# GpSimd's sums of activations split into rows of 384 columns

## The chip, the cores and the metric

The kernel runs on one core of a Trainium2 chip. The metric is the device time of one execution in microseconds; the time before is the median of three runs.

## What is computed

Routing attention, followed by one MLP-mixer block, all in float32:

```
q, k, v: (4, 8, 768, 64); 16 centroids for each head
mask   = argmax(q_n @ c_n) == argmax(k_n @ c_n)          # routed clusters
attn   = softmax(where(mask, q @ k.T / 8, -1e9)) @ v
x      = attn, heads joined                              # (4, 768, 512)
u      = x + (relu(x.T @ w_tok1) @ w_tok2).T             # tokens: 768 -> 256 -> 768
out    = u + relu(u @ w_ch1) @ w_ch2                     # channels: 512 -> 1536 -> 512
```

## The kernel before

The kernel handles 16 pairs of heads (scores, values, place), then the token part of the mixer, then its channel part. The change touches the channel part alone, some 420 us to the end of the span.

**The channel part.** The four batches form two groups of two. For each group channel1 computes the hidden activations and channel2 the output. Both are products of 2 x 2 block matrices done in Strassen's way: seven block products for four, and in each of the seven again seven steps (function product). A step is a product of three blocks of 128 rows, of 384 columns each, on TensorE; each block takes two passes, so a step is six matmul instructions. What the Strassen scheme needs beside that are sums and differences of blocks: of the weights (prepared earlier, kept in DRAM as wd1 and wd2 and loaded through a ring of eight buffers), of the right-hand operand (tsum inside product, combine between products), and of the results (in the drain from PSUM, whose second operand is the sum so far).

**Shapes.** A Mat is a matrix with n rows of 768 columns in each partition; sub(a, c) is one of its four quarters, n/2 rows of 384 columns. The operands of channel1 are quarters of u, with n = 2, so a quarter is one row of 384. The hidden matrices Hm[...] have n = 6, so a quarter is three rows of 384: 1152 elements in each partition.

**Which engine.** Drains of PSUM are on VectorE (tt, line 868) or ScalarE (copy, line 848). The sums in the arena, the one large SBUF tile, go through the same tt: on GpSimd for channel1's sums and for the input sums of channel2's first two products (product is called with sums ("POOL",)), on VectorE for the others. In channel1 the combines of T1 and T2 may go to either engine in the first group. ScalarE applies relu in place (line 875). The function check (lines 1771 to 1804) counts on VectorE whether the inputs were in the fast path's range; it is issued in the program between channel1(1) and channel2(1), and two matmuls of three columns in it stand on TensorE's queue at that place.

**The order.** Every operation is handed to a planner, Program (g.add), with its modelled cost, the keys that it reads and writes (pieces of 32 words of the arena, PSUM banks) and the engines that may take it. TensorE's order is that of the program. For the others, plan repeatedly takes the earliest possible start and, among what an engine can start then, the operation with the earliest due time; due times are computed backwards from TensorE's. VectorE and GpSimd operations that touch no PSUM exclude each other in the model (the field port). Modelled cost is a + b x elements: GpSimd 0.12 + 0.0023 n, VectorE 0.16 + 0.00104 n. Each engine then executes its instructions in that order, with semaphores.

The planner's choice for VectorE, which may start an operation up to 0.15 us after the earliest one that it could start:

```python
                        if s > t + HOLD.get(e, 0.0) + 1e-9:
                            continue
                        ...
                        if pick is None or (o.due, o.seq) < (pick[0].due, pick[0].seq):
                            pick = (o, s)
```

Of the kernel before, what the change touches and what calls it, by code (L numbers as in the profile page):

```python
# [14 lines left out]
ALU = mybir.AluOpType  # L15
# [15 lines left out]
HS = HJ * P  # L31
# [678 lines left out]
def kernel(  # L710
# [112 lines left out]
    def bank(*i):  # L823
        return [("ps", n) for n in i]


    def mm(dst, lhsT, rhs, start, stop, cost, rd, wr, pos=None, tr=None):
        def fn(e):
            nc.tensor.matmul(  # L829
                dst, lhsT=lhsT, rhs=rhs, start=start, stop=stop, tile_position=pos,  # L830
                is_transpose=tr, skip_group_check=True,
            )

        return g.add({"PE": cost}, fn, rd, wr)
# [6 lines left out]
    def cost(kind, n):  # L841
        a, b = COST[kind]
        return a + b * n

    def copy(dst, src, n, rd, wr, engines=("ACT", "DVE")):
        def fn(e):
            if e == "ACT":
                nc.scalar.copy(out=dst, in_=src)  # L848
            else:
                nc.vector.tensor_copy(out=dst, in_=src)  # L850

        return g.add({e: cost(e, n) for e in engines}, fn, rd, wr)
# [13 lines left out]
    def tt(dst, a, b, op, n, rd, wr, engines=("DVE",)):  # L866
        def fn(e):
            (nc.vector if e == "DVE" else nc.gpsimd).tensor_tensor(out=dst, in0=a, in1=b, op=op)  # L868

        return g.add({e: cost(e, n) for e in engines}, fn, rd, wr)  # L870
# [13 lines left out]
    def dma(dst, src, rd, wr, kb, row, after=0.0, queue="SP"):  # L884

        q = {"SP": nc.sync, "ACT": nc.scalar, "POOL": nc.gpsimd}[queue]
        return g.add(
            {queue: ISSUE}, lambda e: q.dma_start(dst, src), rd, wr, (kb * 1024, row), after  # L888
        )
# [667 lines left out]
    def combine(dst, a, b, op, engines=("DVE",)):  # L1557

        n = dst.n // 2
        for i in range(2):  # L1560
            for c in range(2):
                (d, dk), (x, xk), (y, yk) = (z.sub(i, c) for z in (dst, a, b))
                tt(d, x, y, op, n * HS, xk + yk, dk, engines)

    def combine_rows(dst, a, b, op, parts=1):
        n = dst.n // parts
# [4 lines left out]
    def product(which, Q, X, dst, base, sums=None, then=()):  # L1571


        nonlocal nring, nt
        wide = which == 1
        sums = sums or (("POOL",) if wide else ("DVE",))
        ts = (t1s if wide else t2s)[nt % 2]
        nt += 1
        half = X.n // 2
        x = {(a, c): X.sub(a, c) for a in range(2) for c in range(2)}  # L1580

        def tsum(i, a, b):
            tt(ts[i].ap, a[0], b[0], ALU.subtract, half * HS, a[1] + b[1], ts[i].k(), sums)
            return ts[i].ap, ts[i].k()

        T1 = tsum(0, x[0, 1], x[0, 0])
        T2 = tsum(1, x[1, 1], T1)
        T3 = tsum(2, x[1, 1], x[0, 1])
        T4 = tsum(3, x[1, 0], T2)
        if wide:  # L1590
            sets = ((0, 3), (3, 6)) if nset[0] % 2 == 0 else ((3, 6), (0, 3))
        else:
            a = 2 * (nset[1] % 4)
            sets = ((a, a + 1), (a + 1, a + 2))
        nset[0 if wide else 1] += 1

        seq = (
            (0, x[0, 0], 0, True, (0, 0), False), (4, T1, 1, True, (1, 1), False),
            (5, T2, 0, False, (0, 1), False), (2, x[1, 1], 1, False, (0, 1), True),
            (6, T3, 0, False, (1, 1), True), (1, x[1, 0], 1, True, (0, 0), True),  # L1600
            (3, T4, 0, False, (1, 0), False),
        )
        for n, (pn, (r, rk), st, fresh, part, more) in enumerate(seq):
            w = ring[nring % len(ring)]
            nring += 1
            qi = (0, 1, 6, 2, 3, 4, 5)[Q]
            src = wd1[qi, pn] if wide else wd2[qi, pn].rearrange("p a c -> p (a c)")
            dma(
                w.ap.rearrange("p a c -> p (a c)"), src,
                [("wd", which, pn, s) for s in range(6)], w.k(), 192, 1536,  # L1610
            )
            b0, b1 = sets[st]
            for i in range(3):
                bk = b0 + i if wide else b0
                mm(
                    ps[:, bk, 0:HS], w.ap[:, i], r[:, 0] if wide else r[:, i],
                    fresh and (wide or i == 0), wide or i == 2, 0.64, w.k() + rk, bank(bk),
                )
            d, dk = dst.sub(*part)
            src = ps[:, b0:b1, 0:HS]  # L1620
            bks = bank(*range(b0, b1))
            sz = (b1 - b0) * HS
            src_base = dst if more else base
            if src_base is None:
                copy(d, src, sz, bks, dk)
            else:
                y, yk = src_base.sub(*part)
                tt(d, src, y, ALU.add, sz, bks + yk, dk)
            for late in dict(then).get(n, ()):
                late()  # L1630
# [7 lines left out]
    def channel1(grp):  # L1638
        u = {(K, N): Mat(uTs[2 * grp + N], 2 * K, 2) for K in range(2) for N in range(2)}
        Hm = {mn: Mat(t, 0, 6) for mn, t in Hs.items()}  # L1640
        T1, T2, T3, T4 = (Mat(t, 0, 2) for t in TL)
        a, b, c, h11 = Hm[0, 1], Hm[1, 0], Hm[1, 1], Hm[0, 0]
        SUB, ADD = ALU.subtract, ALU.add
        first = ("DVE", "POOL") if grp == 0 else ("POOL",)
        product(1, 0, u[0, 0], h11, None)
        combine(T1, u[0, 1], u[0, 0], SUB, first)
        combine(T2, u[1, 1], T1, SUB, first)
        product(1, 4, T1, c, None)
        product(1, 5, T2, a, h11)
        combine(T3, u[1, 1], u[0, 1], SUB, ("POOL",))  # L1650
        product(1, 6, T3, b, a)
        combine(a, a, c, ADD, ("POOL",))
        combine(c, c, b, ADD, ("POOL",))
        relu_of(c)
        product(1, 1, u[1, 0], h11, h11)
        relu_of(h11)
        product(1, 2, u[1, 1], a, a)
        relu_of(a)
        combine(T4, u[1, 0], T2, SUB, ("POOL",))
        product(1, 3, T4, b, b)  # L1660
        relu_of(b)
# [247 lines left out]
```

## Time and profile before

| | before |
|---|---|
| median of 3 runs | 811.82 us (810.64 to 812.14) |
| profiled execution | 812.03 us, span 810.2 us |
| TensorE busy | 791.3 us, 3743 matmuls |
| VectorE busy | 678.1 us |
| ScalarE busy | 473.0 us |
| GpSimd busy | 178.8 us, 124 instructions |
| mean granted TensorE clock | 0.998 |

The profile calls TensorE PE, VectorE DVE, ScalarE ACT, GpSimd POOL and SyncE SP. A row of the instructions in order of time has the start in us, the duration, the engine, the line, the operation, out<-in, the form (partitions x elements), how many were merged into it and, in brackets, the idle time before it with what ended it. An operation that is held up after its start shows a long duration and no idle time. A row of the busy time by stretch gives the stretch, its length, and for TensorE, its weight loads, VectorE, ScalarE and GpSimd the busy time and the instructions, then the granted clock, the DMA share and GB/s. The span is from the first to the last instruction; the execution's own time is 1.8 us longer.

### The profile page before, as it was taken

What the parts mean: (1) busy time and instruction counts of PE and PEld (TensorE: products, weight loads), DVE (VectorE), ACT (ScalarE), POOL (GpSimd) and SP (SyncE); (2) the same over time, 40 slices, a digit from 0 to 9 for tenths busy, and PEclk for the clock granted to TensorE, in tenths of its full rate; (3) what the DMA queues carried; (4) which work ended last, traced back from release to release, by engine and by line L of the source; (5) the groups of instructions that cost most, each with busy time, mean ns of one, the idle gap of its engine ahead of it and who ended that gap; (6) DMA issues with size and microseconds to landing.
All of it is one profiled execution on the core that took longest, in us unless ns stands there. A gap on an engine that the chain in (4) does not pass through costs nothing.

```text
span 810.2 us, 10859 instructions
## 1 busy us (share of the span) xinstructions
PE 791.3 (98%) x3743; PEld 429.2 (53%) x3743; DVE 678.1 (84%) x873; ACT 473.0 (58%) x612; POOL 178.8 (22%) x124
## 2 busy tenths in 40 slices
PE   5999999999999999999999999999999999999997
PEld 3444445554444445444555555555555555555554
DVE  3789999999999999998898867699975686789984
ACT  3688888888888875699913236433464504400424
POOL 1000000000000000000345398500196379620000
PEclk9999999999999999999999999999999999999999
DMA  5777778879888984369739765556899833333766
GB/s 123 213 181 179 179 195 207 211 181 226 204 210 182 226 236 115 82 132 222 146 85 260 202 199 177 184 176 202 239 252 239 223 109 107 97 96 99 160 156 167
DMA packets 265120, 143.49 MB, mean 177 GB/s; under 512 B 184289, under 2 KB 260961, under 8 KB 265057
## 3 DMA queue, kind: packets, MB, share of 16 engines
q1 hardware_dynamic: 262560, 141.88, 68.7%
q10 hardware_dynamic: 2496, 0.84, 0.4%
q8 instruction: 32, 0.52, 0.3%
q14 instruction: 32, 0.25, 0.1%
HBM read 91.95 MB, written 28.61 MB: 149 GB/s over the span
## 4 chain that ended last, share of the span: by engine, by line
PE 95%; DVE 1%; issue 1%; DMA 0%; ACT 0%; SPq 0%; ACTq 0%
PE ps L829 95%; DVE arena L868 0%; DVE arena L850 0%; DMA arena<-arena 0%; ACT arena L1122 0%; ACT arena L848 0%; SPq L888 0%; DVE arena L1244 0%; DVE arena L1045 0%; DVE arena L1044 0%; ACT arena L1053 0%; DVE arena L1790 0%; ACTq L848 0%
## 5 line engine op out<-in xcount | busy, mean ns | idle before, releaser
L829 PE MATMUL ps<-arena 128*128 128x384 f32 (+6 forms) x3743 | 791.3, 464 | 13.5 <-DVE arena L981 5.7
L829 PEld LDWEIGHTS ps<-arena 128*128 128x128 f32 (+3 forms) x3359 | 409.8, 169 | 349.3 <-issue 143.4
L868 DVE TENSOR_TENSOR arena<-arena 128x1536 f32<-128x1536 f32 (+6 forms) x355 | 369.0, 1064 | 14.8 <-ACT arena L1122 7.3
L868 POOL TENSOR_TENSOR arena<-arena 128x384 f32<-128x384 f32 (+1 forms) x116 | 175.4, 1538 | 534.3 <-DVE arena L868 396.7
L868 DVE TENSOR_TENSOR arena<-ps,arena 128x384 f32<-128x384 f32 (+2 forms) x259 | 207.7, 809 | 79.3 <-PE ps L829 72.0
L858 ACT COPY arena<-arena 128x768 uint16<-128x768 uint16 (+1 forms) x197 | 191.2, 1047 | 45.0 <-DVE arena L868 24.4
L1122 ACT ACTIVATE arena<-ps 128x768 f32<-128x768 f32 x192 | 150.2, 809 | 16.7 <-PE ps L829 13.2
L848 ACT COPY arena<-ps 128x384 f32<-128x384 f32 (+2 forms) x67 | 44.9, 670 | 137.3 <-PE ps L829 127.2
L875 ACT ACTIVATE arena<-arena 128x1152 f32<-128x1152 f32 (+1 forms) x38 | 39.9, 1074 | 56.6 <-DVE arena L868 29.3
L1759 ACT ACTIVATE arena<-arena 128x768 f32<-128x768 f32 x40 | 38.7, 967 | 56.8 <-DMA arena<-in_moe_w_ch_dram 39.9
L829 PEld LDWEIGHTS <-arena 64*128 64x128 bf16 x384 | 19.3, 94 | 26.1 <-issue 1.6
L850 DVE COPY arena<-ps 128x384 f32<-128x384 f32 (+3 forms) x18 | 14.4, 806 | 12.0 <-PE ps L829 10.3
L1044 DVE STREAM_TRANSPOSE arena<-ps 128x384 f32<-128x384 f32 x16 | 9.3, 583 | 15.5 <-PE ps L829 15.5
L1244 DVE SCALAR_TENSOR_TENSOR arena<-arena 128x512 f32<-128x512 uint32 (+1 forms) x31 | 20.7, 691 | 0.2
L1238 DVE SCALAR_TENSOR_TENSOR arena<-arena 128x512 uint32<-128x512 uint32 (+1 forms) x31 | 20.6, 670 | 0.3
L1053 ACT ACTIVATE arena<-arena 128x384 bf16<-128x384 f32 x16 | 11.2, 703 | 10.3 <-DVE arena L1179 10.3
L1241 DVE TENSOR_SCALAR arena<-arena 128x512 uint32<-128x512 uint32 (+1 forms) x31 | 12.7, 429 | 0.2
L1234 DVE TENSOR_SCALAR arena<-arena 128x512 uint32<-128x512 uint32 (+1 forms) x31 | 12.9, 437 | 0.0
L1049 DVE STREAM_TRANSPOSE arena<-arena 128x384 f32<-128x384 f32 x16 | 9.2, 575 | 0.4
L1045 DVE TENSOR_REDUCE arena<-arena 128x24 f32<-128x384 f32 x16 | 8.8, 553 | 0.6
L1759 ACT ACTIVATION_READ_ACCUMULATOR arena<-arena 128x1 f32 x40 | 7.5, 189 | 0.0
L1186 DVE RECIPROCAL arena<-arena 128x12 f32<-128x12 f32 x16 | 3.6, 228 | 0.5
(47 smaller groups left out, 21.4 us busy)
## 6 DMA issues: line engine op xcount, KB each, us to landing
arena<-wd SPq DMA_DIRECT2D x196, 192.0 KB, 2.4
wd<-arena SPq DMA_DIRECT2D x84, 224.0 KB, 3.9
arena<-in_moe_w_ch_dram SPq DMA_DIRECT2D x48, 256.0 KB, 4.5
arena<-in_moe_w_ch_dram SPq DMA_DIRECT2D x16, 768.0 KB, 4.4
arena<-in_v_dram SPq DMA_DIRECT2D x16, 384.0 KB, 4.4
out_dram<-arena SPq DMA_DIRECT2D x14, 384.0 KB, 3.7
arena<-in_k_dram SPq DMA_DIRECT2D x13, 384.0 KB, 4.3
arena<-in_q_dram SPq DMA_DIRECT2D x13, 384.0 KB, 4.5
```

What stands on the lines that cost most here:

```text
L829: nc.tensor.matmul(dst, lhsT=lhsT, rhs=rhs, start=start, stop=stop, tile_position=pos, is_transpose=tr, skip_group_check=True,)
L848: nc.scalar.copy(out=dst, in_=src)
L850: nc.vector.tensor_copy(out=dst, in_=src)
L858: nc.scalar.copy(out=dst, in_=src)
L868: (nc.vector if e == "DVE" else nc.gpsimd).tensor_tensor(out=dst, in0=a, in1=b, op=op)
L875: nc.scalar.activation(out=dst, in_=src, func=ACT.Relu)
L1122: lambda e, ex=ex, s=s: nc.scalar.activation(out=ex.ap, in_=ps[:, 2 * s : 2 * s + 2, 0:HS], func=ACT.Exp, scale=SM_SCALE),
L1234: vec(lambda: nc.vector.tensor_scalar(out=hh, in0=hi, scalar1=0x07FFFFFF, scalar2=3, op0=ALU.bitwise_and, op1=ALU.logical_shift_left,), f, ...
L1238: vec(lambda: nc.vector.scalar_tensor_tensor(out=TT, in0=hi, scalar=0xC0000000, in1=hh, op0=ALU.bitwise_and, op1=ALU.bitwise_or), 0.14 + 0 ...
L1241: vec(lambda: nc.vector.tensor_scalar(out=hh, in0=TT, scalar1=0xFF800000, scalar2=None, op0=ALU.bitwise_and), f, T.k(), h.k())
L1244: vec(lambda: nc.vector.scalar_tensor_tensor(out=ll, in0=lo, scalar=float(2.0**-52), in1=hh.bitcast(F32), op0=ALU.mult, op1=ALU.mult,), 0. ...
L1759: lambda e, i=i, func=func, bias=bias, n=n, hi=hi: nc.scalar.activation(out=hi, in_=hi, func=func, bias=bias, accum_out=wsum.ap[:, i, n : ...
```

## The change

A sum whose only possible engine is GpSimd is issued row by row: one operation for each row of 384 columns, where a quarter of a hidden matrix was one operation of 1152. Each row's operation states the keys of the whole quarters that it reads, and the keys of the one row that it writes. The sums of u, with quarters of one row, and those that VectorE does or may do stay as they were. Since the planner gets other operations with other costs, the order of the other engines' instructions can come out differently too.

```diff
@@ combine
         for i in range(2):
             for c in range(2):
                 (d, dk), (x, xk), (y, yk) = (z.sub(i, c) for z in (dst, a, b))
-                tt(d, x, y, op, n * HS, xk + yk, dk, engines)
+                w = 1 if engines == ("POOL",) else n
+                for r in range(0, n, w):
+                    tt(
+                        d[:, r : r + w], x[:, r : r + w], y[:, r : r + w], op, w * HS,
+                        xk + yk, dst.buf.rows(
+                            dst.r0 + i * n + r, dst.r0 + i * n + r + w, c * HS, (c + 1) * HS
+                        ), engines,
+                    )
@@ product
         def tsum(i, a, b):
-            tt(ts[i].ap, a[0], b[0], ALU.subtract, half * HS, a[1] + b[1], ts[i].k(), sums)
+            n = 1 if sums == ("POOL",) else half
+            for r in range(0, half, n):
+                tt(
+                    ts[i].ap[:, r : r + n], a[0][:, r : r + n], b[0][:, r : r + n],
+                    ALU.subtract, n * HS, a[1] + b[1], ts[i].rows(r, r + n), sums,
+                )
             return ts[i].ap, ts[i].k()
```

## The prediction

> **What bounds the kernel now.** I read the page first: the busy times and the chain that ended last.
>
> ```profile
> span 810.2 us, 10859 instructions
> ...
> PE 791.3 (98%) x3743; PEld 429.2 (53%) x3743; DVE 678.1 (84%) x873; ACT 473.0 (58%) x612; POOL 178.8 (22%) x124
> ...
> PE 95%; DVE 1%; issue 1%; DMA 0%; ACT 0%; SPq 0%; ACTq 0%
> ```
>
> TensorE is the bound: 791.3 of 810.2 us, and 95% of the chain. GpSimd, the engine that the change touches, is busy for 178.8 us and does not stand in the chain. The change leaves TensorE's work alone, so it can only move the time through moments at which TensorE stands idle. The second view is therefore the list of TensorE's own waits (total, times, longest), here whole, and with it the busy time by stretch of 50 us, of which two rows fall short of 50 after the start:
>
> ```profile
> PE ps L829 <- DVE arena L981: 5.7, 1, 5.7
> PE ps L829 <- issue: 1.6, 1, 1.6
> PE ps L829 <- DVE arena L868: 1.6, 2, 1.2
> PE ps L829 <- DVE arena L850: 1.2, 2, 0.9
> PE ps L829 <- DMA arena<-in_k_dram: 0.9, 1, 0.9
> PE ps L829 <- DMA arena<-arena: 0.9, 1, 0.9
> PE ps L829 <- ACT arena L848: 0.9, 2, 0.8
> PE ps L829 <- ACT arena L1122: 0.6, 1, 0.6
> ```
>
> ```profile
> 650.00:700.00 50.00, 48.75 (x151) 28.36 (x150) 37.16 (x32) 13.41 (x12) 39.96 (x21) 1.00 0.38 108
> 700.00:750.00 50.00, 48.41 (x152) 28.16 (x151) 44.80 (x44) 6.57 (x8) 11.43 (x4) 1.00 0.34 96
> ```
>
> GpSimd is in no line: TensorE never waits for one of its sums directly. Between 350 and 800 us TensorE has only two holes, 1.25 us before 661 and 1.59 us before 712 (50.00 less 48.75, and less 48.41). Both lie where GpSimd runs its wide sums. The third view, instructions in order of time, shows each. First hole:
>
> ```profile
> 657.23 3.58 POOL L868 TENSOR_TENSOR arena<-arena 128x1152 f32<-128x1152 f32 x2
> ...
> 656.12 1.36 DVE L868 TENSOR_TENSOR arena<-ps,arena 128x1152 f32<-128x1152 f32 x1 [0.58 <-PE ps L829]
> 657.40 2.49 DVE L1790 TENSOR_SCALAR arena<-arena 128x20 f32<-128x20 f32 x1
> 659.80 2.61 DVE L868 TENSOR_TENSOR arena<-ps,arena 128x1152 f32<-128x1152 f32 x2
> ...
> 661.20 0.59 PE L829 MATMUL ps<-arena 128*128 128x384 f32 x1 [1.25 <-DVE arena L868]
> ```
>
> VectorE's tiny test of 20 columns (L1790, in check) takes 2.49 us. It starts 0.17 us after a wide GpSimd sum and ends with it. VectorE's next drain of PSUM begins only then, and TensorE has run dry. So an operation of VectorE that reads and writes the arena alone stands still until GpSimd's current operation is over, while a drain from PSUM does not: the wide drain takes 1.36 us beside GpSimd too. Second hole:
>
> ```profile
> 702.19 11.51 POOL L868 TENSOR_TENSOR arena<-arena 128x1152 f32<-128x1152 f32 x4 [4.45 <-PE ps L829]
> ...
> 707.36 6.34 POOL L868 TENSOR_TENSOR arena<-arena 128x1152 f32<-128x1152 f32 x2
> ...
> 706.17 1.41 DVE L868 TENSOR_TENSOR arena<-ps,arena 1x3 f32<-1x3 f32 x2 [0.73 <-PE ps L829]
> 707.51 3.71 DVE L868 TENSOR_TENSOR arena<-arena 128x1152 f32<-128x1152 f32 x1
> 711.14 1.01 DVE L868 TENSOR_TENSOR arena<-ps,arena 128x384 f32<-128x384 f32 x2
> ...
> 705.90 2.36 PE L829 MATMUL ps<-arena 128*32 128x3 f32 x8
> ...
> 711.79 0.56 PE L829 MATMUL ps<-arena 128*128 128x384 f32 x1 [1.59 <-issue]
> ```
>
> A sum of VectorE in channel2(1) starts 0.15 us after a wide GpSimd sum and takes 3.71 us instead of some 1.36. Two drains of 384 columns queue behind it. The third step of TensorE's product reuses the first drain's bank and starts at 711.79, about 0.1 us after that drain (711.14 plus half of 1.01). The page says "issue" there; I read it as this drain.
>
> **The change part by part.** Of GpSimd's sums 32 are wide, and only these are split: 16 in channel1's two GpSimd combines on the hidden activations (2 x 4 in each of two groups) and 16 in the input sums of channel2's first two products (2 x 4 in each group). The sums over u have rows of 384 already.
>
> ```profile
> L868 POOL TENSOR_TENSOR arena<-arena 128x384 f32<-128x384 f32 x84 | 90.0, 1090 | 513.5 <-DVE arena L868 394.2 <-PE ps L829 116.0 <-DMA wd<-arena 2.9
> L868 POOL TENSOR_TENSOR arena<-arena 128x1152 f32<-128x1152 f32 x32 | 86.3, 2713 | 20.8 <-PE ps L829 14.2 <-DVE arena L868 2.6 <-DVE arena L1786 2.3
> ...
> 389.19 4.00 POOL L868 TENSOR_TENSOR arena<-arena 128x384 f32<-128x384 f32 x4 [385.25 <-DVE arena L868]
> 399.78 1.96 POOL L868 TENSOR_TENSOR arena<-arena 128x384 f32<-128x384 f32 x2 [6.60 <-DVE arena L868]
> ```
>
> So 32 operations become 96: the count of 116 goes to 180.
>
> *GpSimd's own time.* Two rows in a row take 1.96 us, so one more costs 0.96 and three take 2.9 to 3.0. A wide sum takes 2.6 (11.51 us for four has one turn of VectorE in it; the group's mean is 2.71). A split adds 0.3, and 32 splits some 10 us of GpSimd. By the mean of all narrow sums, 1.09, it is 3.27 less 2.71, or 18 us. [...]
>
> What hides this: GpSimd works well ahead. In the second group
>
> ```profile
> 692.51 5.23 POOL L868 TENSOR_TENSOR arena<-arena 128x1152 f32<-128x1152 f32 x2 [2.10 <-PE ps L829]
> ```
>
> ends the four sums of channel2's first product at 697.74, and TensorE starts that product after the eight matmuls at 705.90, whose first two are check's. Twelve splits lie before that point, at most 12 x 0.57 = 6.8 us by the dearest price and 3.6 by mine, against 8.2 of lead. The last four sums are released by TensorE at 702.19 and end at 713.70; 2.3 us later is 716.0, and the product that reads them starts seven steps of 1.93 us after 706.1, at 719.6. I cost this at nothing. Should the lead be eaten, the rest of these microseconds would be paid.
>
> *First hole.* With rows, the operation that VectorE's small test meets is at most 1.0 us long. Wherever in a row it starts, 657.40 + 1.0 + 0.1 = 658.5 at the latest. The drain then ends by 659.86, before TensorE runs dry at 659.96 (661.20 less 1.25). So all of 1.25 us goes, in every phase; the other bound is nothing, if the plan puts something else there.
>
> *Second hole.* VectorE's sum started 0.09 us after GpSimd's second wide sum (end 707.42), so I take it that it waits for that. As six rows, these two end near 702.19 + 6 x 0.96 = 707.95, half a microsecond later. GpSimd goes straight on to its next row, so VectorE is held for 0 to 0.96 us: start 708.0 to 708.9, end 709.4 to 710.3, first drain until 709.9 to 710.8, TensorE 0.1 later. It runs dry at 710.20 (711.79 less 1.59), so 0 to 0.7 us of the hole is left. I take 0.25 us, half a row of holding; 1.34 us goes. If VectorE drains first (that bank is full at about 708.3, close by), nothing is left.
>
> *The planner.* The kernel orders itself by modelled costs. There a wide sum costs 0.12 + 0.0023 x 1152 = 2.77 and a row 1.00, and VectorE's and GpSimd's arena operations exclude each other. New costs and finer turns give new due times and so another order on VectorE, GpSimd, ScalarE and SyncE; the transfers move with it. Where it matters is narrow: the stretches with wide GpSimd sums. In the first group's, up to channel2 (464 to 516 us), VectorE has just one arena operation:
>
> ```profile
> L868 DVE TENSOR_TENSOR arena<-ps,arena 128x1152 f32<-128x1152 f32 x27 | 36.7, 1358 | 15.1 <-PE ps L829 15.1
> L868 DVE TENSOR_TENSOR arena<-arena 128x448 f32<-128x448 f32 x1 | 0.6, 616 | 0.0
> ```
>
> I take 0 for the new order. Its bounds are -0.25 (what I left of the second hole) and +5.4 (twice 2.7, the slower rival below).
>
> *Sum.* 1.25 + 1.34 = 2.59 us off the profiled execution's 812.03 us (span 810.2, 1.8 around it): **809.4 us**. That execution lies 0.2 us above the median of 811.82.
>
> **The rivals.**
>
> *One hole stays.* The plan may again set a VectorE sum ahead of a drain that TensorE needs, held by a row or two. Then 812.03 - 1.25 = 810.8, or with both holes in another place 812. For it: the second hole's cure depends on 0.7 us. Against it: the first is cured in any phase. Chance 0.20. A hole of about 1 us in a new place with both old ones gone gives 810.4 and is counted here.
>
> *VectorE takes turns that drains need: slower.* In the model the arena comes free for VectorE each 1.0 us and not each 2.8, so the planner can start a VectorE sum in a gap in which it formerly held VectorE for the drain. The place is the start of channel2, where VectorE is busy for 44.80 of 50 us. A drain there has a margin of 710.20 - 708.3 - 0.5 = 1.4 us; one sum of 1.36 ahead of it costs nothing, three cost 3 x 1.36 - 1.4 = 2.7 each time. Paid once (with both old holes gone: 812.03 - 2.84 + 2.7) it gives 811.9, no difference; in both groups 814.6. So it decides from the second place on. For it: group two shows that one held sum makes a hole. Against it: most VectorE sums there wait for GpSimd or TensorE, and VectorE loses less to holding. Chance of the slower form 0.26, of the one-place form 0.03.
>
> *GpSimd starves.* Where both engines sum, narrow GpSimd operations lose a turn each:
>
> ```profile
> 585.06 8.20 POOL L868 TENSOR_TENSOR arena<-arena 128x384 f32<-128x384 f32 x5 [62.45 <-PE ps L829]
> ```
>
> That is 1.64 us for each of five. Twelve rows from 702.19 would end at 721.9; at a full turn each (0.96 + 1.36) at 730. The fourth sum is used in the seventh step, at 719.6 + 6 x 1.93 = 731.2. So even this ends just in time and gives 809.4; only with more than a turn for each row does it add about a microsecond, 810.5. Chance 0.03. The Trainium skill (SBUF — State Buffer, "SBUF: two separate sides") says that the pair of ports which VectorE and GpSimd share is locked for a whole instruction and that the loser blocks fully; the rows above agree in both directions, and by it more and shorter GpSimd operations mean more lost turns as well as shorter holds.
>
> **How the numbers follow.** Forecast 0.48, one hole or a new one 0.20, one-place turns 0.03, starving 0.03, slower 0.26. About 0.2% (1.6 us) is what a measurement of this kernel can tell from no change, so faster means under 810.2 and slower over 813.4. The forecast's own range is 808.9 (both holes gone, 809.2, less the 0.2 between the profiled execution and the median, rounded) to 810.1 (0.7 of the second hole left, 809.9, and 0.2 of spread). Nearly all of it is faster; with a few hundredths from the edge of the second case: faster 0.50, same 0.24, slower 0.26. Both signs are in play, so the range over all cases goes from 808.8 to 815.0: above it stay the orders with a third bad place, below it nearly nothing.
>
> **What would show it.** Right: 180 narrow-sized GpSimd operations and no wide ones, GpSimd busy for 187 to 197 us; L1790 under 1.1 us; no VectorE arena sum of 1152 columns above 2.4 us; TensorE's holes near 660 and 711 gone, the stretch from 650 to 750 at 99.5 or more. Wrong: a TensorE wait of over 1 us for VectorE at the start of channel2 in either group, with two or more VectorE sums ahead of the drain; or TensorE waiting for GpSimd at all, which would mean that the lead of 8 us was eaten.

## The result and the profile after

| | before | after |
|---|---|---|
| median of 8 executions | 812.03 us | 808.73 us (807.14 to 809.03) |
| ratio to before | | 0.9955, 95% interval 0.9945 to 0.9965 |
| profiled execution | 812.03 us, span 810.2 | 808.70 us, span 806.9 |

One of the eight executions before took 1197.51 us, the others 810.64 to 812.14; the ratios here leave such strays out. The change makes the kernel faster by 0.45%. The sign is the forecast one; the size is not, and 808.73 lies just below the range, whose lower end was 808.8.

The page of the changed kernel, busy times and GpSimd's group; then the stretches of 50 us in which TensorE had its two holes (TensorE's busy time first, its weight loads, VectorE, ScalarE, GpSimd):

```profile
span 806.9 us, 10917 instructions
...
PE 790.8 (98%) x3743; PEld 429.4 (53%) x3743; DVE 673.3 (83%) x874; ACT 472.1 (59%) x611; POOL 187.9 (23%) x188
...
L868 POOL TENSOR_TENSOR arena<-arena 128x384 f32<-128x384 f32 x180 | 184.6, 1065 | 522.9 <-DVE arena L868 398.6 <-PE ps L829 120.8 <-DMA wd<-arena 2.9
```

```profile
650.00:700.00 50.00, 50.00 (x156) 29.39 (x155) 36.16 (x31) 13.52 (x12) 45.47 (x48) 1.00 0.39 109
700.00:750.00 50.00, 50.00 (x157) 29.31 (x156) 43.56 (x47) 8.61 (x11) 10.57 (x10) 1.00 0.37 102
```

Both holes are gone, GpSimd has 180 narrow sums and 8.3 us more of them (184.6 less 90.0 and 86.3). Matching the 3743 matmuls of both traces one by one shows where the time went: their starts agree within 0.05 us up to the first hole. The first matmul behind it starts 1.40 us earlier and all that follow 1.51; behind the second hole it is 3.26 for the first and 3.34 from the next one to the end. So the first hole was worth 1.51 us and the second 1.83. Nothing else moved TensorE.

But VectorE in order of time does not show what the prediction described. The small test of 20 columns (now line 1802) and the start of channel2:

```profile
640.07 0.17 DVE L1802 TENSOR_SCALAR arena<-arena 128x20 f32<-128x20 f32 x1
...
704.66 1.41 DVE L868 TENSOR_TENSOR arena<-ps,arena 1x3 f32<-1x3 f32 x2 [0.73 <-PE ps L829]
706.79 0.56 DVE L868 TENSOR_TENSOR arena<-ps,arena 128x384 f32<-128x384 f32 x1 [0.72 <-PE ps L829]
708.73 0.56 DVE L868 TENSOR_TENSOR arena<-ps,arena 128x384 f32<-128x384 f32 x1 [1.38 <-PE ps L829]
709.20 1.40 DVE L868 TENSOR_TENSOR arena<-arena 128x1152 f32<-128x1152 f32 x1
710.66 0.56 DVE L868 TENSOR_TENSOR arena<-ps,arena 128x384 f32<-128x384 f32 x1
711.14 1.54 DVE L868 TENSOR_TENSOR arena<-arena 128x1152 f32<-128x1152 f32 x1
```

The test runs at 640, far from the sums that held it at 657. In channel2 the first two drains now stand ahead of VectorE's first arena sum; before, that sum stood ahead of them. So the planner's order changed at exactly the two places that mattered, and two theories fit the result. A, shorter holds: a VectorE operation is held for one GpSimd operation, which is now 1.0 us long and not 2.6. B, the new order: the held operations were moved out of the way.

### The profile page after: what moved, and what is told of

Same layout as the page of the kernel before. It is cut to its first block, busy times and chain, and to the rows that moved or that the text cites. A ratio compares the mean times of both kernels' runs of the same rounds, so it can differ in the third digit from the quotient of the medians.

```text
span 806.9 us, 10917 instructions
## 1 busy us (share of the span) xinstructions
PE 790.8 (98%) x3743; PEld 429.4 (53%) x3743; DVE 673.3 (83%) x874; ACT 472.1 (59%) x611; POOL 187.9 (23%) x188
## 4 chain that ended last, share of the span: by engine, by line
PE 96%; DVE 1%; DMA 0%; ACT 0%; issue 0%; SPq 0%; ACTq 0%
PE ps L829 96%; DVE arena L850 0%; DMA arena<-arena 0%; DVE arena L868 0%; ACT arena L1122 0%; ACT arena L848 0%; SPq L888 0%; DVE arena L1244 0%; DVE arena L1045 0%; DVE arena L1044 0%; ACT arena L1053 0%; ACTq L848 0%
## 5 line engine op out<-in xcount | busy, mean ns | idle before, releaser
L868 POOL TENSOR_TENSOR arena<-arena 128x384 f32<-128x384 f32 x180 | 184.6, 1065 | 522.9 <-DVE arena L868 398.6
```

## The experiments

A planner makes the two easy to separate: what it is told of a sum and what is then issued need not agree. Each kernel was timed against the kernel before on its own chip. "Old order" below means that VectorE, ScalarE and SyncE have the order of the kernel before, operation for operation; "new order", that of the changed kernel.

**Old order, rows.** The planner sees one sum of 1152; three rows are issued.

```diff
     def tt(dst, a, b, op, n, rd, wr, engines=("DVE",)):
         def fn(e):
-            (nc.vector if e == "DVE" else nc.gpsimd).tensor_tensor(out=dst, in0=a, in1=b, op=op)
+            if e == "DVE" or n != 3 * HS:
+                (nc.vector if e == "DVE" else nc.gpsimd).tensor_tensor(out=dst, in0=a, in1=b, op=op)
+                return
+            for r in range(3):
+                nc.gpsimd.tensor_tensor(
+                    out=dst[:, r : r + 1], in0=a[:, r : r + 1], in1=b[:, r : r + 1], op=op
+                )
```

> The planner still sees the wide sums of the kernel before, so the order on VectorE, ScalarE and SyncE is that of before; each of the 32 wide GpSimd sums is issued as three rows. Theory A, shorter holds: VectorE's test of 20 columns and its sum at the start of channel2 are held by at most one row, 1.0 us, so the hole near 660 goes whole and 0 to 0.7 us of the one near 711 is left; time about 809, ratio to before 0.996 to 0.997. Theory B, the new order: what removed the holes was that VectorE's test and sum stand elsewhere, and in the old order both are still in the way; time 811 to 812, ratio 0.999 to 1.000.

Measured: 808.95 us, ratio 0.9961 (0.9947 to 0.9975). VectorE in order of time, at the two places:

```profile
658.15 0.19 DVE L1796 TENSOR_SCALAR arena<-arena 128x20 f32<-128x20 f32 x1
658.81 1.36 DVE L869 TENSOR_TENSOR arena<-ps,arena 128x1152 f32<-128x1152 f32 x1 [0.47 <-PE ps L829]
...
706.75 1.79 DVE L869 TENSOR_TENSOR arena<-arena 128x1152 f32<-128x1152 f32 x1
708.46 0.54 DVE L869 TENSOR_TENSOR arena<-ps,arena 128x384 f32<-128x384 f32 x1
```

The test stands at its old place and takes 0.19 us for 2.49; the sum stands ahead of the drain as before and takes 1.79 for 3.71. TensorE has no hole at either. One more rival falls with these rows, that rows let VectorE's operations start sooner because their data are ready sooner: both start where they did in TensorE's work. The test is 0.75 us later than in the trace of before, as are TensorE's matmuls there, and the sum 0.76 us earlier, again as they are. Only the time that they take has changed. Theory A holds; the shorter operations alone bring nearly the whole gain. Matched matmul by matmul with before, this kernel wins 1.51 us at the first hole and 1.83 at the second, and loses 0.25 near 518, where a VectorE sum is now held for 0.6 us.

**New order, wide sums.** The reverse: the planner sees rows, and one of a sum's three places issues the whole.

```diff
-    def tt(dst, a, b, op, n, rd, wr, engines=("DVE",)):
+    def tt(dst, a, b, op, n, rd, wr, engines=("DVE",), whole=None):
         def fn(e):
+            if whole:
+                if whole[0] is not None:
+                    nc.gpsimd.tensor_tensor(out=whole[0], in0=whole[1], in1=whole[2], op=op)
+                return
```

(whole holds the three operands at the third row and None at the others.)

> The planner sees the rows of the changed kernel, so the order on VectorE, ScalarE and SyncE is that of the changed kernel; on GpSimd the first two rows of each sum issue nothing and the third issues the whole sum of 1152. Theory A, shorter holds: with the long operations back, the two VectorE sums from 709 us on are held for up to 2.6 us, the drain behind them comes late and a hole of 1 to 2 us opens there; time 809.7 to 811, ratio 0.997 to 0.999. Theory B, the new order: no hole comes back, since the test runs at another time and the drains that TensorE needs stand ahead of the sums; time within 0.5 us of the changed kernel's 808.7, ratio 0.9955.

Measured: 812.78 us, ratio 1.0015 (1.0005 to 1.0025), with holes of 1.55 us at 509, 1.50 at 701 and 0.83 at 717. It does not answer the question. The third row is not always the last in the planner's order, so a whole sum can be issued ahead of reads of what its buffer held before; this kernel computes other values, and its waits are other ones: ahead of 511 and 702 TensorE waits for GpSimd itself. The next kernel counts the three places and issues the sum at the last of them:

```diff
+            if whole:
+                whole[0] -= 1
+                if whole[0] == 0:
+                    nc.gpsimd.tensor_tensor(out=whole[1], in0=whole[2], in1=whole[3], op=op)
+                return
```

> As in the run with the new order and wide sums, but a sum is issued whole at whichever of its three rows the planner placed last, so that it never stands ahead of a read of what its buffer held before. VectorE, ScalarE and SyncE have the order of the changed kernel. Theory A, shorter holds: the hole near 660 stays away, because the test of 20 columns has moved; from 709 us on a VectorE sum is held for up to 2.6 us again and a hole of 0.5 to 2 us opens behind it; time 809.2 to 811, ratio 0.9965 to 0.999. Theory B, the new order alone: no hole, time 808.2 to 809.1, ratio 0.9955.

Measured: 811.94 us, ratio 0.9991 (0.9982 to 1.0). VectorE, then TensorE in order of time:

```profile
709.96 3.10 DVE L873 TENSOR_TENSOR arena<-arena 128x1152 f32<-128x1152 f32 x1
712.99 0.55 DVE L873 TENSOR_TENSOR arena<-ps,arena 128x384 f32<-128x384 f32 x1
713.46 3.31 DVE L873 TENSOR_TENSOR arena<-arena 128x1152 f32<-128x1152 f32 x1
716.69 0.54 DVE L873 TENSOR_TENSOR arena<-ps,arena 128x384 f32<-128x384 f32 x1
```

```profile
713.64 2.17 PE L829 MATMUL ps<-arena 128*128 128x384 f32 x6 [0.32 <-issue]
717.33 0.88 PE L829 MATMUL ps<-arena 128*128 128x384 f32 x2 [1.52 <-issue]
```

The two sums that took 1.40 and 1.54 us with rows take 3.10 and 3.31, the drains behind them are late, and TensorE stands still twice. The hole near 660 stays away, since the test has moved; one of 0.68 us opens near 522. Matched with the changed kernel, whose order it shares, the three cost 3.24 us; A had counted on one hole only, and 811.94 lies above its 809.2 to 811. The new order by itself is worth 0.1%, by the interval 0.2% at most. Theory B falls as a cause of the gain, though it did remove the first hole in its own way.

**One half of the change at a time**, each being one of the two hunks of the change as it stands, with the planner free (its order then differs from both kernels).

> Rows in combine alone (16 of the 32 wide sums, those beside the hole near 660). Theory A, shorter holds: the hole near 660 goes (1.4 us), the one near 711, beside the wide input sums, stays (1.8 us); time about 810.6, ratio 0.998. Theory B, the new order: each part is its own draw of the planner, and which holes there are doesn't follow the part; anything from 808.7 to 812, and a hole may go that has no rows beside it or come at a new place.

Only the edit of combine: 810.19 us, 0.9982 (0.9971 to 0.9992). VectorE, and the stretch from 700:

```profile
704.60 3.71 DVE L868 TENSOR_TENSOR arena<-arena 128x1152 f32<-128x1152 f32 x1
708.23 1.01 DVE L868 TENSOR_TENSOR arena<-ps,arena 128x384 f32<-128x384 f32 x2
```

```profile
700.00:750.00 50.00, 48.41 (x152) 28.22 (x151) 45.56 (x45) 6.93 (x10) 10.70 (x4) 1.00 0.34 99
```

The second hole stands as it was, 1.59 us, as A said.

> Rows in the input sums of product alone (the other 16, those beside the hole near 711). Theory A, shorter holds: the hole near 711 goes (1.8 us), the one near 660 stays (1.4 us); time about 810.2, ratio 0.998. Theory B, the new order: a draw of its own, 808.7 to 812, and a hole may go that has no rows beside it or come at a new place.

Only the edit of product: 809.48 us, 0.9969 (0.9959 to 0.9979), about 0.7 us better than A's 810.2. Both holes are gone, also the one near 660 where the sums are still wide:

```profile
648.03 0.17 DVE L1795 TENSOR_SCALAR arena<-arena 128x20 f32<-128x20 f32 x1
```

The test had moved to 648, ahead of the wide sums. So here B's part of the expectation came true: each new plan puts this test elsewhere, and in all three it was out of harm's way. To see the first hole's price without that, the same half in the old order (combine passes a flag to tt, and rows are issued only with it; this edit and the next two are shown against the kernel of old order and rows):

```diff
-            if e == "DVE" or n != 3 * HS:
+            if e == "DVE" or n != 3 * HS or not rows:
```

> Order of the kernel before; of the 32 wide sums only the 16 of combine are issued as rows. Theory A, shorter holds, with a hole's cost counted from start to start: the hole near 660 goes, worth 1.41 us, the one near 711 stays; span 1.4 us shorter, time about 810.6, ratio 0.998, and the stretch from 700 to 750 is short of 50 by some 1.6 us. Theory B, the new order: both holes stay, ratio 1.000.

Measured: 810.95 us, 0.9984 (0.9975 to 0.9992). The hole near 660 is gone; the stretch from 700 has 48.41 us. Against the trace of before, TensorE's first matmul after 660 has gained 1.41 us and all that follow 1.51, and the second hole is paid in full. A, nearly in its numbers: 810.95 us for about 810.6.

**How narrow?** Old order again, other pieces in place of the row. Two pieces of 3 x 192:

```diff
-            for r in range(3):
-                nc.gpsimd.tensor_tensor(
-                    out=dst[:, r : r + 1], in0=a[:, r : r + 1], in1=b[:, r : r + 1], op=op
-                )
+            for c in range(0, HS, HS // 2):
+                s = slice(c, c + HS // 2)
+                nc.gpsimd.tensor_tensor(out=dst[:, :, s], in0=a[:, :, s], in1=b[:, :, s], op=op)
```

> Order of the kernel before; each wide sum is issued as two operations of 3 x 192 columns, 576 in all, about 1.35 us each by 0.14 + 0.0021 n. Holds of at most 1.4 us: the test near 657.4 ends by 658.9, the drain behind it by 660.2, so a hole of 0 to 0.3 us is left near 660 and 0 to 0.9 us near 711; time 809 to 809.6, ratio 0.996 to 0.997, a little worse than three rows or equal to them.

Measured: 809.53 us, 0.9971 (0.996 to 0.9982). The test takes 1.40 us and leaves a hole of 0.16 near 660; near 711 there is none. As expected. Six pieces of 192:

```diff
             for r in range(3):
-                nc.gpsimd.tensor_tensor(
-                    out=dst[:, r : r + 1], in0=a[:, r : r + 1], in1=b[:, r : r + 1], op=op
-                )
+                for c in range(0, HS, HS // 2):
+                    nc.gpsimd.tensor_tensor(
+                        out=dst[:, r, c : c + HS // 2], in0=a[:, r, c : c + HS // 2],
+                        in1=b[:, r, c : c + HS // 2], op=op,
+                    )
```

> Order of the kernel before; each wide sum is issued as six operations of 192 columns. By the rows a sixth takes about 0.5 us (0.96 for 384 columns and 0.82 for 384 more give 0.14 + 0.0021 n = 0.55), so a sum takes 3.3 us for 2.6, and the 12 sums ahead of channel2 in a group 8 us longer, as much as the lead that I counted. Theory A, shorter holds: no hole near 660 and 711, time 808.5 to 809.2, as with three rows, since halving a hold of 1 us buys nothing more. The rival that the lead is eaten: TensorE waits for GpSimd at the start of channel2, 1 us or more, time 810 to 812.

Measured: 820.1 us, 1.0127 (1.0092 to 1.0162). Both sides were wrong. VectorE, GpSimd and TensorE in order of time at the start of channel2:

```profile
705.37 8.84 DVE L869 TENSOR_TENSOR arena<-arena 128x1152 f32<-128x1152 f32 x1
714.13 1.01 DVE L869 TENSOR_TENSOR arena<-ps,arena 128x384 f32<-128x384 f32 x2
...
705.77 8.88 POOL L873 TENSOR_TENSOR arena<-arena 128x192 f32<-128x192 f32 x14
...
714.78 0.98 PE L829 MATMUL ps<-arena 128*128 128x384 f32 x1 [6.72 <-POOL arena L873]
```

The lead was not eaten: channel2's first product had its sums in time. Instead VectorE's sum was held for 7.5 us, through fourteen GpSimd operations in a row; it started only when GpSimd had none left but one. The profile writes TensorE's 6.72 us down to GpSimd; I put them down to the drain behind the held sum, which ended at 714.68. TensorE's queue stood in a wait that names VectorE's semaphore until 714.73; in the trace of before the same wait ended at 711.73, behind a drain that ended at 711.69. Yet in the first group of the same trace such a sum was held for one operation of 192 only:

```profile
514.49 1.70 DVE L869 TENSOR_TENSOR arena<-arena 128x1152 f32<-128x1152 f32 x1
```

So a hold is not always one operation long. GpSimd's operations overlap a little in the trace (they start every 0.55 us and take 0.58 to 0.66), and in the second group this overlap had grown from 0.04 to 0.11 us in a run of some 50 us without a pause. Two theories of what keeps VectorE out were tried: that overlap, and the shortness. One kernel issues the four input sums of channel2's second product in pieces of 192 and all other wide sums as rows (the edit below, piece being the width that tt issues); the other has HS and HS // 2 exchanged. These four are not quite the last four of the group, as the expectations have it: GpSimd takes sums of the two products in turns, and one of the first product's stands among the last four. The two at the end are of the second product.

```diff
         def tsum(i, a, b):
-            tt(ts[i].ap, a[0], b[0], ALU.subtract, half * HS, a[1] + b[1], ts[i].k(), sums)
+            tt(ts[i].ap, a[0], b[0], ALU.subtract, half * HS, a[1] + b[1], ts[i].k(), sums,
+               HS // 2 if which == 2 and Q == 0 else HS)
```

> Order of the kernel before; rows of 384 for all wide sums but the last four of each group (the input sums of channel2's second product), which are issued in six operations of 192 each. They begin after a pause of GpSimd, so consecutive operations should overlap by only 0.04 us at first. Theory C, overlap: VectorE gets its turn between two GpSimd operations while they overlap by 0.05 us or less and loses it when a long run without a pause has let them overlap by 0.1 us; here VectorE's sum near 707 is held for under 1 us, no hole, time about 809, ratio 0.996. Theory D, shortness: operations of 192 columns follow each other so fast that VectorE never gets in; the sum near 707 is held for most of the 24 operations, 7 us or more, and TensorE has a hole of 4 to 8 us there, time 813 to 820.

Measured: 808.79 us, 0.9956 (0.9942 to 0.997), no hole; VectorE's sum near 706 took 1.57 us and the one near 709 1.69, both among operations of 192. Shortness falls.

> The reverse of the run before: operations of 192 columns for all wide sums but the last four of each group, which are rows of 384. GpSimd then comes to the last four out of a run of some 50 us almost without a pause. Theory C, overlap: the operations overlap by about 0.1 us by then, and VectorE's sum near 707 is held through several rows, 3 us or more; a hole of 2 to 7 us near 711, time 811 to 818. Theory D, shortness: rows of 384 let VectorE in after at most 1.0 us; no hole near 711, time about 809.

Measured: 814.05 us, 1.0019 (1.0006 to 1.0032). VectorE, GpSimd, TensorE:

```profile
709.72 5.65 DVE L869 TENSOR_TENSOR arena<-arena 128x1152 f32<-128x1152 f32 x1
...
708.40 5.76 POOL L873 TENSOR_TENSOR arena<-arena 128x384 f32<-128x384 f32 x6
...
715.94 8.29 PE L829 MATMUL ps<-arena 128*128 128x384 f32 x20 [2.86 <-issue]
```

A hole there, as the overlap theory said, and in the range of its time; but not for its reason. VectorE's first sum, near 707, still met a sum in pieces of 192 and was held for 0.12 us; it is the next one, at 709.72, that met the rows. The rows that kept VectorE out overlapped by just 0.04 us, and at 516 in the same trace a VectorE sum got in between two operations that overlapped by 0.12. So the overlap falls too. The same trace has a third case, a sum held for 1.27 us near 523, through the rest of one row and the whole of the next:

```profile
523.02 2.61 DVE L869 TENSOR_TENSOR arena<-arena 128x1152 f32<-128x1152 f32 x1
...
522.45 1.96 POOL L873 TENSOR_TENSOR arena<-arena 128x384 f32<-128x384 f32 x2
```

In all three VectorE got in only as GpSimd's run came to its end, with one operation left or none. All three have more than 50 us of GpSimd work without a pause ahead of them, which the kernels with rows or halves do not have; but in those long runs VectorE also got in several times after a single operation. The single executions of these two kernels differ more than those of the others (818.1 to 827.5 us and 810.4 to 815.6, against 2 to 3.5 us), so the length of the hold may change from one execution to the next; one of each was traced. What decides it stays open.

## Why the prediction was right or wrong

- **The bound and the two holes: right.** They were all there was to gain, and TensorE is 3.34 us earlier at the end for them alone.
- **GpSimd's own time: right.** 10 us expected, 8.3 measured, hidden; TensorE waits for no GpSimd sum. One reading in it was wrong and cost nothing: the sums that end at 697.74 are not yet all of channel2's first product, whose fourth runs from 704.78 to 707.42 (the order of the two products' sums shows where they are issued in different widths, as in the last two experiments); that one is used only in the seventh step, some 10 us later.
- **First hole: right in size of effect, and by another road.** It went whole. The mechanism as predicted (the test meets a row of 1.0 us) is what the old order with rows shows, 0.19 us for 2.49. In the changed kernel the test wasn't there to be held.
- **Second hole: the 0.25 us that I left was not there.** Neither in the changed kernel, whose drains go first, nor in the old order with rows, where the sum was held for 0.4 us. The step behind it, that this sum waits for GpSimd's second wide sum and so starts at 708.0 at the earliest, was wrong: in the old order with rows it starts at 706.75, as the drain ahead of it on VectorE ends, while the last row of GpSimd's second sum still runs (until 707.32).
- **The price of a hole: here the sum failed.** The step "1.25 + 1.34 = 2.59" took a hole to be TensorE's idle time. The chain pays from start to start. In the trace of before, the last matmul ahead of each hole and the second one behind it (the first one behind it stands in the prediction, at 661.20 and 711.79):

```profile
659.47 0.49 PE L829 MATMUL ps<-arena 128*128 128x384 f32 x1
661.63 0.49 PE L829 MATMUL ps<-arena 128*128 128x384 f32 x1
...
709.71 0.49 PE L829 MATMUL ps<-arena 128*128 128x384 f32 x1
712.19 0.49 PE L829 MATMUL ps<-arena 128*128 128x384 f32 x1
```

  Matmuls take 0.49 us but start every 0.32. After 659.47 the next one was due at 659.79 and came at 661.20, 1.41 us late, and the one behind it came 0.11 later than its pace: 1.52, not 1.25. After 709.71 it was due at 710.03 and came at 711.79, 1.76 us late, and the one behind it 0.08 later than its pace: 1.84, not 1.59. The matched matmuls have 1.51 and 1.83. So the sum had the holes 0.26 and 0.24 us too small, and with the 0.25 left over the missing 0.75 us is accounted for: 2.59 + 0.75 = 3.34. The range's lower end inherited the same error, since it took both holes at their idle time.
- **The planner at 0: right as a sum, wrong as a picture.** The order changed at both places; alone it is worth 0.1%, at most 0.2%, beside the rows nothing that these runs can tell (0.9955 against 0.9961, intervals overlapping).
- **The rivals.** No hole stayed, and no drain lost its turn. GpSimd did not starve. The danger that the experiments found was not among them: that VectorE starves behind GpSimd's operations, which happened in neither the kernel before nor the changed one. "At most 1.0 us" for a hold was taken as a law and is none, as the two kernels with 5.65 and 8.84 us show; it held in the changed kernel and in those next to it.

The Trainium skill (SBUF — State Buffer, "SBUF: two separate sides") has the shared pair of ports locked for a whole instruction; that agrees with every hold of one operation here. By it the operation that starts first has the pair; it does not say which of two that wait gets it next, and the sum of 8.84 us started ahead of thirteen of the fourteen operations that it stood behind.

## What to carry to other kernels

Where TensorE is the bound, price a hole from the start of one matmul to the start of the next less the usual pace, not by the idle time between them. A small VectorE operation can cost as much as the GpSimd operation that it meets, so look for operations whose duration is far above their group's usual and see what ran beside them; splitting the long partner into pieces of about 1 us removed the wait for 8 us of GpSimd time that nobody missed, where pieces of 0.55 us made this kernel 1.3% slower. And when a planner orders the kernel, separate what the planner is told from what is issued, before crediting either.

## What the runs showed of the hardware

*VectorE can be held for many GpSimd operations*, and not for one: the sums of 8.84, 5.65 and 2.61 us above took 1.34 unheld. Unsettled.

*A hole of some microseconds costs more than itself.* In the kernel with sixths and in that with rows last, the stretches behind the holes of 6.7 and 2.9 us (the column before the last two is TensorE's granted clock):

```profile
714.70:717.00 2.30, 2.22 (x4) 1.34 (x5) 1.71 (x2) 0.00 (x0) 0.00 (x0) 0.50 0.00 0
```

```profile
716.00:718.00 2.00, 2.00 (x4) 1.09 (x5) 0.50 (x1) 0.00 (x0) 0.00 (x0) 0.50 0.00 0
```

TensorE comes back at half its clock (0.50): its matmuls start every 0.64 us for a while, which costs another 2.8 us after the long hole and 1.7 after the short one. Behind the holes of 1.25 and 1.59 us of before the clock is 1.00. The Trainium skill (TensorE: Matmul & The Clock Gate, "What's actually happening") has the clock drop after an idle window of about 3.4 us; here a hole of 2.9 us, 3.35 from start to start, was enough.

*The start varies by more than this change's uncertainty.* From 11 to 16 us, before and in the kernel with the edit of combine alone, which is the same there:

```profile
11.00:16.00 5.00, 5.00 (x26) 2.95 (x20) 2.27 (x4) 1.99 (x4) 0.00 (x0) 1.00 0.14 46
```

```profile
11.00:16.00 5.00, 4.68 (x36) 2.62 (x40) 2.27 (x4) 2.39 (x5) 0.00 (x0) 1.00 0.13 47
```

TensorE gets through 36 instructions for 26, and all that follows is 1.3 us earlier. Executions of one kernel fall into two groups about as far apart (807.14 to 807.46 and 808.70 to 809.03 for the changed kernel); that the start is what parts them was not traced. So spans of single traces were compared here only from matmul to matmul.
